# Longer convolution blocks, a reordered first load and two-instruction mixes in a convolution plus channel-mix kernel

## The chip, the cores and the metric

The kernel runs on one core of one Trainium2 chip. The metric is the device time of that core in microseconds (us), less is better. An execution counts as "fast" or "slow" by its state. The granted clock that is quoted for an execution is the mean share of full TensorE speed that the throttle allowed; in a single stretch it is 1.00 or 0.50.

## The reference

There are B = 8 batches of S = 4160 tokens with D = 192 channels. First a causal convolution over 7 taps, whose weights are softmaxed and shared by the 24 channels of each of 8 heads; then a channel mix with a hidden width of 1024.

```python
w = softmax(weight, axis=-1)                       # 8 heads x 7 taps
y[b, s, h*24+g] = sum_k w[h, k] * x[b, s + k - 6, h*24+g]
y_prev = y shifted by one token (zero at the start)
xk = mu_k * y + (1 - mu_k) * y_prev
xr = mu_r * y + (1 - mu_r) * y_prev
k = relu(xk @ w_k) ; v = (k * k) @ w_v             # 192 -> 1024 -> 192
out = sigmoid(xr @ w_r) * v
```

## The kernel before

The batches are worked in four pairs. The convolution is a matmul on TensorE: a block of 112 tokens and its halo of 6 earlier ones lies on the partitions of `xb`, and for every head one Toeplitz matrix `toe` with the seven weights on its diagonals multiplies it. Several blocks form a group. The tiles that matmuls write (`ps_...`) lie in PSUM, a memory apart from that of the other tiles. ScalarE evicts the result to `y` in bf16. `y` has tokens on its partitions and must be turned, so that channels are there: the first four groups of pair 0 go through TensorE transposes (`ps_t`, copied to `yT` by VectorE), all later ones through memory and a transposing DMA.

```python
BLK = 112 ; GB = 10 ; WARM = 34 ; P = 128 ; G = 24     # NBLK = 38 blocks a pair

# groups: (blocks, the step that needs them, turned on TensorE?)
((3, 0, True), (4, 1, True), (5, 2, True), (4, 3, True), (10, 4, False), (6, 6, False), (6, 7, False))
if p == 0
else ((10, 0, False), (10, 2, False), (9, 4, False), (9, 6, False))

def conv_mm(g, c, pool=None, tag="m"):
    ...
    ps = (pool or psM).tile([P, nb, 2, G * len(hs)], FP32, tag=tag, name="ps_c")   # psM holds two tiles
    for i, h in enumerate(hs):
        nc.tensor.matmul(out=ps[:BLK, :, :, i * G : (i + 1) * G], lhsT=toe[:, h, :],
                         rhs=xbs[g][:, :nb, :, h * G : (h + 1) * G], start=True, stop=True)
```

The main work is cut into steps of 512 tokens and, finer, into 260 slots. A slot is one k tile: 4 matmuls of 512 columns (8 of 256 in the short first and last step of pair 0) into `ps_k`, a ReLU eviction of 128x1024 by ScalarE (`k_sb`, 1.02 us), a square on VectorE (0.68 us). Beside it in each slot run matmuls of v and r of an earlier step. Pair 0 has slots 0 to 64, each later pair 65 more. The start of each `k_sb` eviction is the clock by which two traces can be laid side by side, and this text uses it so: "slot 12 is 0.72 us ahead" means that the 13th `k_sb` starts 0.72 us earlier than in the kernel before.

Between `yT` and k lies VectorE's part: a difference `d` of neighbouring tokens, then each mix as one instruction.

```python
nc.vector.scalar_tensor_tensor(out=o, in0=d[r0:r1, sl, :L], scalar=mu[r0:r1, i, part:part+1],
                               in1=yT[r0:r1, sl, c0:c0+L], op0=ALU.mult, op1=ALU.add)
```

The prologue warms TensorE with idle matmuls, writes the softmaxed rows to memory (`w_scr`) and reads them back diagonally as `toe`. DMAs named `nc.gpsimd` are issued by GpSimd, one after another.

```python
load_x(0) ; load_x(1)
nc.gpsimd.affine_select(out=ident, ...)
for _ in range(WARM): nc.tensor.matmul(out=warm, lhsT=ones_t, rhs=zeros, ...)
softmax()
nc.sync.dma_start(out=w_scr, in_=w_row)
load_toe() ; load_wk() ; load_x(2) ; load_wr() ; load_wv()
...
for t in tails: nc.gpsimd.memset(t, 0.0)
conv_mm(0, ...) ; conv_out(0, ...) ; tr_mm(0, ...) ; tr_out(0, ...)
conv_mm(1, ...) ; conv_out(1, ...)
diff(0) ; mix(0, ...) x4
for j in range(2): tr_mm(1, j) ; tr_out(1, j, dve_)
```

Later work stands in tables by slot. For groups turned on TensorE:

```python
per = 1
c0 = n0 - 14 if n0 > 12 else 1     # first convolution
r0 = c0 + nc_ + 1                  # first transpose; nc_ convolution pieces
```

## Time and profile before

| | before |
|---|---|
| median of six executions | 468.72 us (468.38 to 469.89) |
| profiled span | 467.2 us |
| TensorE busy (PE) | 445.2 us, 95% |
| VectorE busy (DVE) | 390.4 us, 84% |
| ScalarE busy (ACT) | 374.6 us, 80% |
| first convolution starts | 13.19 us |
| first `k_sb` starts | 20.90 us |
| granted clock 0.50 | 14.58 to 21.40 us |

TensorE is the bound of the steady state, and the first 20 us are a chain of waits with hardly any main work. The prediction below shows the lines.

### The profile page before, as it was taken

To read this page: it belongs to the slowest core of one execution; us is meant where nothing else is said; L and a number is where in the kernel's file an instruction comes from. 1 tells how busy PE (TensorE), PEld (TensorE's weight loads), DVE (VectorE), ACT (ScalarE), POOL (GpSimd) and SP (SyncE) were. 2 spreads that over 40 slices of the span, in tenths; PEclk is the share of its full clock that TensorE was granted. 3 is DMA by queue.
4 is the path that set the end of the run, shared out by engine and by line. 5 is a ranking of instruction groups with operands and counts; after the bars stand their busy time and mean duration, and the time that the engine had idled before them with its cause. 6 is when DMAs were issued, how large, how long until landed. Compare 5 with 4: busy or idle time off the path is not lost.

```text
span 467.2 us, 9868 instructions
## 1 busy us (share of the span) xinstructions
PE 445.2 (95%) x3892; PEld 300.6 (64%) x3954; DVE 390.4 (84%) x616; ACT 374.6 (80%) x549; POOL 51.1 (11%) x71
## 2 busy tenths in 40 slices
PE   7788999999999999999999999999999999999996
PEld 3454766666776666666676666666676666666676
DVE  2778988797998879889798989978898987999873
ACT  2489888988879797888879788888978888777771
POOL 5812211000010041000002041000002000000000
PEclk9799999999999999999999999999999999999999
DMA  7996699972459599945367679937157753511222
GB/s 89 160 174 106 162 197 156 233 200 68 127 142 183 148 139 229 181 129 139 93 173 119 165 133 214 229 100 187 52 152 138 173 135 100 153 65 56 69 69 94
DMA packets 138942, 65.79 MB, mean 141 GB/s; under 512 B 89936, under 2 KB 138464, under 8 KB 138896
## 3 DMA queue, kind: packets, MB, share of 16 engines
q1 hardware_dynamic: 98000, 49.26, 41.0%
q0 software_dynamic: 40896, 15.90, 30.0%
q8 instruction: 31, 0.51, 0.4%
q14 instruction: 15, 0.12, 0.1%
HBM read 31.59 MB, written 37.52 MB: 148 GB/s over the span
## 4 chain that ended last, share of the span: by engine, by line
PE 91%; ACT 2%; issue 2%; DMA 2%; DVE 1%; DVEq 0%; ACTq 0%
PE ps_k L343 38%; PE ps_v L433 37%; PE ps_c L199 5%; PE ps_r L416 5%; PE ps_r L415 5%; ACT k_sb L372 1%; DMA w_scr<-w_row 1%; PE ps_k L360 1%; DMA toe<-w_scr 1%; ACT y L219 1%; DMA w_raw<-in_weight_dram 1%; PE ps_t L257 1%; DVE yT L268 0%; ACT y L222 0%; DVE k L391 0%
## 5 line engine op out<-in xcount | busy, mean ns | idle before, releaser
L372 ACT ACTIVATE k_sb<-ps_k 128x1024 bf16<-128x1024 f32 x260 | 260.2, 1026 | 35.8 <-PE ps_k L343 31.8
L343 PE MATMUL ps_k<-xk,wk 64*128 64x512 bf16 (+2 forms) x994 | 206.0, 376 | 9.5 <-ACT k_sb L372 0.9
L433 PE MATMUL ps_v<-wv,k 128*128 128x192 bf16 x2048 | 210.8, 246 | 0.0
L433 PEld LDWEIGHTS <-k 128*128 128x128 bf16 x2048 | 175.4, 98 | 30.6 <-issue 1.4
L391 DVE TENSOR_TENSOR k<-k_sb 128x1024 bf16<-128x1024 bf16 x256 | 174.8, 684 | 16.7 <-ACT k_sb L372 16.0
L343 PEld LDWEIGHTS <-wk 64*128 64x128 bf16 (+1 forms) x1056 | 56.2, 96 | 109.2 <-issue 107.9
L446 DVE TENSOR_TENSOR o_sb<-ps_v,r_sb 128x384 f32<-128x384 f32 x132 | 72.2, 547 | 39.6 <-PE ps_v L433 34.7
L423 ACT ACTIVATE r_sb<-ps_r 128x384 bf16<-128x384 f32 x132 | 64.3, 487 | 38.1 <-PE ps_r L416 37.3
L301 DVE SCALAR_TENSOR_TENSOR xr<-d,mu,yT 128x1024 bf16<-128x1024 bf16 (+1 forms) x66 | 65.1, 988 | 0.1
L301 DVE SCALAR_TENSOR_TENSOR xk<-d,mu,yT 128x1024 bf16<-128x1024 bf16 (+1 forms) x66 | 64.4, 977 | 0.2
L415 PE MATMUL ps_r<-wr,xr 128*128 128x192 bf16 x256 | 62.8, 246 | 0.0
L416 PE MATMUL ps_r<-wr,xr 128*128 128x192 bf16 x256 | 62.8, 246 | 0.0
L219 ACT CAST y<-ps_c 112x480 bf16<-112x480 f32 (+4 forms) x100 | 47.9, 483 | 10.4 <-PE ps_c L199 10.2
L199 PE MATMUL ps_c<-xb,toe 128*112 128x480 bf16 (+5 forms) x152 | 46.2, 332 | 5.3 <-DMA toe<-w_scr 2.9
L109 POOL DMA_DIRECT2D xb<-in_x_dram x38 | 34.9, 928 | 26.8 <-PE ps_c L199 15.9
L281 DVE TENSOR_TENSOR d<-yT 128x1536 bf16<-128x1536 bf16 (+2 forms) x37 | 31.8, 859 | 0.4 <-DMA yT<-y_dram 0.2
L108 POOL DMA_DIRECT2D xb<-in_x_dram x8 | 4.3, 538 | 215.7 <-PE ps_k L343 206.3
L199 PEld LDWEIGHTS <-toe 128*112 128x112 bf16 x152 | 19.2, 134 | 12.1 <-DMA toe<-w_scr 3.4
L222 ACT CAST y<-ps_c 112x480 bf16<-112x480 f32 (+8 forms) x53 | 25.2, 482 | 0.2 <-DVE yT L227 0.2
L415 PEld LDWEIGHTS <-xr 128*128 128x128 bf16 x256 | 25.0, 98 | 0.0
L416 PEld LDWEIGHTS <-xr 128*128 128x128 bf16 x256 | 25.0, 98 | 0.0
L103 POOL DMA_DIRECT2D xb<-in_x_dram x8 | 4.6, 581 | 62.4 <-PE ps_r L416 61.0
(46 smaller groups left out, 67.8 us busy)
## 6 DMA issues: line engine op xcount, KB each, us to landing
out_dram<-o_sb SPq DMA_DIRECT2D x128, 192.0 KB, 2.3
y_dram<-y SPq DMA_DIRECT2D x7, 840.0 KB, 5.0
xb<-in_x_dram POOLq DMA_DIRECT2D x12, 432.0 KB, 12.0
y_dram<-y SPq DMA_DIRECT2D x6, 756.0 KB, 4.6
xb<-in_x_dram POOLq DMA_DIRECT2D x8, 480.0 KB, 13.2
xb<-in_x_dram POOLq DMA_DIRECT2D x6, 384.0 KB, 6.6
y_dram<-y SPq DMA_DIRECT2D x2, 504.0 KB, 10.7
xb<-in_x_dram POOLq DMA_DIRECT2D x4, 240.0 KB, 5.3
```

Source lines behind the costliest of these rows:

```text
L109: nc.gpsimd.dma_start(out=xb[:, lo:hi, s, :], in_=bass.AP(tensor=x.tensor, offset=x.offset + (b * S + t0 + lo * BLK) * D, ap=[[D, P], [BLK ...
L199: nc.tensor.matmul(out=ps[:BLK, :, :, i * G : (i + 1) * G], lhsT=toe[:, h, :], rhs=xbs[g][:, :nb, :, h * G : (h + 1) * G], start=True, sto ...
L219: copy(out=yh[:, :, :, c0 : c0 + n], in_=ps[:BLK, :, :, 0:n])
L301: nc.vector.scalar_tensor_tensor(out=o, in0=d[r0:r1, sl, :L], scalar=mu[r0:r1, i, part : part + 1], in1=yT[r0:r1, sl, c0 : c0 + L], op0=AL ...
L343: nc.tensor.matmul(out=ps[:, i, f * L : (f + 1) * L], lhsT=wk[r, 0 if hi else 1, fs], rhs=xk[r, i if hi else 2, :L], start=start and f == ...
L372: nc.scalar.activation(out=k_sb, in_=ps.rearrange("p a b -> p (a b)"), func=AF.Relu)
L391: nc.vector.tensor_tensor(out=o, in0=i, in1=i, op=ALU.mult)
L415: nc.tensor.matmul(out=o, lhsT=hi, rhs=wr[:, 0, :], start=True, stop=False)
L416: nc.tensor.matmul(out=o, lhsT=lo, rhs=wlo, start=False, stop=True)
L423: nc.scalar.activation(out=r_sb[:, :n, :], in_=ps[:, :n, :], func=AF.Sigmoid)
L433: nc.tensor.matmul(out=o, lhsT=k2[:, f, t * P : (t + 1) * P], rhs=wv[:, f, :], start=(f == 0), stop=(f == NF - 1),)
L446: nc.vector.tensor_tensor(out=o_sb[:, :n, :], in0=v_ps.pop(m)[:, :n, :], in1=r_sbs.pop(m)[:, :n, :], op=ALU.mult)
```

## The change

The intent: blocks of 120 tokens waste less of the 128 partitions on halo, so a pair needs 35 blocks, not 38. The Toeplitz matrix gets 128 columns. The second group's `x` is read behind the Toeplitz matrix instead of in front of it. Each mix becomes a scaling (tensor_scalar) and an in-place addition (tensor_tensor). The groups and the slots of the early transposes are rearranged, and six warm-up matmuls are added.

```diff
-    BLK = 112
+    BLK = 120
-    WARM = 34
+    WARM = 40
-            ((3, 0, True), (4, 1, True), (5, 2, True), (4, 3, True), (10, 4, False), (6, 6, False), (6, 7, False))
+            ((3, 0, True), (4, 1, True), (4, 2, True), (5, 3, True), (10, 4, False), (6, 6, False), (3, 8, False))
-            else ((10, 0, False), (10, 2, False), (9, 4, False), (9, 6, False))
+            else ((10, 0, False), (8, 2, False), (8, 4, False), (9, 6, False))
-    toe = const.tile([P, H, BLK], BF16)
+    toe = const.tile([P, H, P], BF16)
-                out=ps[:BLK, :, :, i * G : (i + 1) * G],
+                out=ps[:, :, :, i * G : (i + 1) * G],
@@ mix
-        elif part == 0:
-            go(t[:, 0:2, :L], slice(0, 2), 0, P)
         else:
-            go(t[:, 2, :L], 2, 0, P)
+            sl = slice(0, 2) if part == 0 else slice(2, 3)
+            o = t[:, sl, :L]
+            nc.vector.tensor_scalar(
+                out=o, in0=d[:, sl, :L], scalar1=mu[:, i, part : part + 1], scalar2=None, op0=ALU.mult
+            )
+            nc.vector.tensor_tensor(out=o, in0=o, in1=yT[:, sl, c0 : c0 + L], op=ALU.add)
@@ schedule
-            r0 = c0 + nc_ + 1
+            r0 = c0 + nc_
@@ prologue
         load_x(0)
-        load_x(1)
...
         load_toe()
+        load_x(1)
         load_wk()
```

Cut here: the padding of `yT` to a multiple of 16, the clipping of the transposing read at S, and the width of the Toeplitz read.

## The prediction

> **What bounds the kernel now.** I read the page's busy shares first, then the chain that ended last, then the same engines stretch by stretch, and last the chain and the timeline of the first 23 us.
>
> ```profile
> PE 445.2 (95%) x3892; PEld 300.6 (64%) x3954; DVE 390.4 (84%) x616; ACT 374.6 (80%) x549; POOL 51.1 (11%) x71
> PE 91%; ACT 2%; issue 2%; DMA 2%; DVE 1%; DVEq 0%; ACTq 0%
> ```
>
> TensorE is busy 95% of 467.2 us and carries 91% of the chain. VectorE at 84% is near, so the average alone doesn't say whether VectorE's part of the change can pay. The windows table (busy us of each engine in a stretch) does:
>
> ```profile
> 0.00:13.20 13.20, 8.95 (x35) 3.68 (x35) 2.39 (x10) 3.02 (x4) 8.27 (x17) 1.00 0.75 101
> 13.20:19.30 6.10, 4.55 (x38) 3.64 (x39) 4.23 (x10) 2.73 (x8) 6.07 (x10) 0.61 1.34 171
> 19.30:43.00 23.70, 19.86 (x152) 11.37 (x155) 20.10 (x31) 19.59 (x33) 7.20 (x10) 0.96 1.03 127
> ...
> 131.00:240.35 109.35, 107.05 (x938) 72.17 (x954) 95.63 (x149) 92.62 (x134) 9.84 (x12) 1.00 0.76 153
> ```
>
> Columns are PE, PEld, DVE, ACT, POOL, then granted clock, DMA share and GB/s. The last row is one pair of batches in the steady state: PE 107.05 of 109.35, VectorE 95.63, so there only TensorE's own work counts. In 19.3 to 43 all three compute engines are near 20 of 23.7: a start-up stage with mixed limits. Before 19.3 nothing of the main work runs; what sets that part is the chain:
>
> ```profile
> 5.21 4.21 DMA w_scr<-w_row
> 9.42 0.29 issue
> 9.71 3.44 DMA toe<-w_scr
> 13.15 0.04 issue
> 13.19 0.60 PE ps_c L199 x6
> ...
> 16.10 0.49 PE ps_c L199 x2
> ...
> 18.35 1.11 PE ps_t L257 x10
> 19.46 1.41 PE ps_k L343 x8
> 20.88 0.02 issue
> 20.90 1.02 ACT k_sb L372
> ```
>
> The softmaxed weights go out to memory (4.21 us) and come back as the Toeplitz matrix (3.44 us); from the first convolution to the first large matmul are about 6 us more, of alternating convolution, eviction and transposition. The DMA records say why the write takes 4.21 us: its 2048-byte packets run from about 7.2 to 8.9 us, while the x packets of group 1 run from 6.4 to 10.2 us beside them.
>
> **What the Trainium skill says.** "VectorE: DVE Perf Modes", section "The perf-mode tier table", puts tensor_scalar on bf16 in SBUF at four elements a cycle (693 ns for 2048) and tensor_tensor at two (1224 ns). For tensor_tensor this trace agrees: the square of 1024 elements takes 684 ns, the difference of 1536 takes 956 ns, which is half the elements at 0.96 GHz plus about 0.15 us. The trace holds no tensor_scalar. The present mix (scalar_tensor_tensor) takes 1279 ns for 1024 and 735 for 512, 1.06 ns an element: one a cycle.
> "TensorE: Matmul & The Clock Gate", section "Weight-path perf modes", says the fast weight load is on when the number of weights is 128. The trace fits: loads of toe with 112 columns take 134 ns, loads of 128 columns 98 ns.
> The same page, section "Part 1: The HAM clock gate", says TensorE falls to half rate after an idle window of about 3.4 us. Here the warm-up matmuls end at 10.3, toe lands at 13.15, and the granted clock is 0.5 from 14.6 to 21.4 us, two such windows; the 8 matmuls of 192 columns at 16.1 took 1.44 us.
>
> **The change part by part.**
> (1) Blocks of 120. A pair of batches needs 35 blocks in place of 38. Every block costs 2 x 192 = 384 streamed columns, so 3 x 4 x 384 = 4608 columns go. In the steady chain the convolution matmul of 432 columns stands with 0.18 us, so 0.417 ns a column: 4608 x 0.417 = 1.92 us, of which 0.48 us in each pair. This is on the path wherever TensorE is the bound, which is nearly everywhere past 43 us. I book -1.9.
> (2) Weight loads of toe with 128 columns: 152 x 36 ns = 5.5 us off PEld. In the steady chain the matmuls follow one another with no gap for the load (k for 1.51 us, convolution 0.18, v at once), so it is hidden. I book 0.
> (3) Mixes. By the skill's four a cycle and the trace's fixed 0.15 us, I estimate a tensor_scalar of 1024 at 256/0.96 + 150 = 0.42 us and of 512 at 0.28. The addition takes 0.68 and about 0.42. Consecutive independent instructions on VectorE start some 0.08 us before the last one's recorded end, dependent ones 0.04 after it. So 1024: before 1.20 a piece, after 0.42 + 0.04 + 0.60 = 1.06; 512: before 0.66, after 0.28 + 0.04 + 0.34 = 0.66. A step of 512 tokens holds two of each: 2 x 0.14 = 0.3 us saved of some 12 us VectorE work, about 9 us in the 31 full steps. In the steady state VectorE waits for TensorE anyway: 0 there. In start-up, where the chain passes an xr mix at 39.95, perhaps 0.2. VectorE's busy time should come out near 380 to 388.
> (4) Group 1's x behind the Toeplitz matrix. Without x packets beside them, 128 packets of 2048 B at 0.09 us on 16 engines are under 0.8 us in place of 1.7. So w_scr should land at about 8.5 (not 9.42) and toe, issued at 8.8, with rows of 256 B in place of 224 B, at about 12.2 to 12.4 (not 13.15): -0.9 up to here. The price: both x transfers of group 1 are issued by 11.5, and their 1024 packets need some 2.4 us at the rate of the trace (about 220 in half a microsecond) after toe's data at 11.8, so they land near 15. The second convolution would want them at 16.1 - 0.9 = 15.2. That is tight: a delay of up to 0.7 is possible. The wk load moves behind them and lands near 17.9, and the first large matmul wants it at 18.4. I book -0.7 with these chances in it.
> (5) Warm-up 40 in place of 34: 6 x 0.213 = 1.3 us more, to 11.6. They end before toe lands, so they delay nothing, and the idle gap shrinks from 2.9 to about 0.7 us. If the clock stays at full rate, 10 transposes (1.11) and 8 k matmuls (1.41) on the chain halve: 1.2 us. But between 12 and 18 us TensorE is busy less than half the time, so another window may count as idle. I give it 4 in 10: -0.5.
> (6) Groups 2 and 3 swap four and five blocks, transposes come one slot earlier. ScalarE's evictions of group 2 shrink by a fifth (five copies, about 0.3 us) in slots 2 to 5, where the chain runs through its k_sb, and grow again in group 3. I book -0.3 with the 0.2 of (3), and see it as the least certain.
> Sum: -1.9 - 0.7 - 0.5 - 0.3 = -3.4, so 468.9 - 3.4 = 465.5 us.
>
> **The rivals.**
> (a) tensor_scalar with a per-partition scalar in memory does not get the fast mode. At one element a cycle it costs 1.22 us for 1024 and 0.69 for 512. Per step VectorE would gain 2 x (1.22 + 0.04 + 0.60 - 1.20) + 2 x (0.69 + 0.04 + 0.34 - 0.66) = 2.1 us, on some 11.7; a step of TensorE is 13.3. VectorE becomes the bound: 13.8 a step, some 33 x 0.5 = 16 us more, about 482. For it: no run here shows the instruction. Against it: the skill's table, and the fixed mode rule that tensor_tensor obeys here.
> (b) The prologue's gain is eaten by the wait that takes its place: x of group 1 or wk lands late and the first k matmul starts at 19.3 or later. For it: GpSimd issues one DMA after another from 10 to 22 us without a pause, and all use one queue. Against it: the x transfers keep 3 us of slack before the second convolution. Time: about 466.7.
> (c) The clock stays up through the whole prologue and start-up loses its knots: another 1.5 us, about 463.5.
> (d) The convolution columns saved don't shorten the chain, because VectorE or ScalarE sets the step. For it: VectorE is busy 87% of the steady window. Against it: TensorE is busy 98% there. Time: 467.4.
>
> **Range and chances.** The convolution's 1.9 is firm. The rest is between +0.3 and -3.5, so 462.9 to 467.3 should hold it 8 times in 10. The 2% marks are at 459.5 and 478.3. Going below the first needs 6 us more than the sum and I see no source; going above the second needs rival (a). Chances: faster 0.03, same 0.94, slower 0.03.
>
> **What would show it.** Right: PE busy in a steady pair falls from 107.05 by about 0.5, and the pair lasts about 108.8; toe lands near 12.3; the first k matmul starts at 18.2 to 18.8; tensor_scalar of 1024 takes near 0.42 us and VectorE's total falls slightly. Wrong: tensor_scalar near 1.2 us with waits of TensorE for xk; a wait of the second convolution for the x DMA beyond 0.7 us; a steady pair still at 109.3; or a w_scr write that still takes over 4 us with no x traffic beside it, so that contention was not its cause.

## More of the kernel before

One caution for all readings of busy time: the ends of matmuls are modelled, and of the 1056 k matmuls this trace holds records of 994. So the starts of `k_sb`, which are recorded on ScalarE, are the safer measure of progress.

## The result, and the profile after

| | before | after |
|---|---|---|
| median of six executions | 468.72 us (468.38 to 469.89) | 466.12 us (465.89 to 466.96) |
| ratio (95% interval) | | 0.9946 (0.9932 to 0.996) |
| profiled span | 467.2 us | 464.4 us |

A ratio is the mean time of one kernel's fast runs over that of the other's of the same rounds, so it is not quite the ratio of the medians. The change saves about half a per cent: "same" by the 2% mark, 0.6 us from the predicted 465.5 and inside the range.

The page of the kernel after, its busy line and the shares of the chain that ended last:

```profile
PE 445.4 (96%) x3898; PEld 298.3 (64%) x3960; DVE 387.3 (83%) x748; ACT 371.3 (80%) x544; POOL 49.5 (11%) x71
PE 91%; DMA 2%; DVE 2%; ACT 2%; issue 2%; POOL 0%; DVEq 0%
```

Nothing changed in kind: TensorE still carries 91%. VectorE lost 3.1 us of busy time while it got 132 more instructions.

The start in the same stretches as before (columns: PE, PEld, DVE, ACT, POOL busy; granted clock, DMA share, GB/s):

```profile
0.00:13.20 13.20, 11.03 (x51) 5.00 (x52) 2.93 (x12) 4.08 (x7) 8.58 (x18) 1.00 0.58 83
13.20:19.30 6.10, 4.50 (x35) 3.10 (x37) 5.28 (x14) 1.69 (x5) 4.30 (x8) 0.61 1.37 192
19.30:43.00 23.70, 19.57 (x153) 11.01 (x153) 19.36 (x36) 20.52 (x34) 5.40 (x7) 0.96 0.98 123
```

PE has 2.08 us more in the first row, the six extra warm-up matmuls and a convolution that now begins inside it. The clock column stands at 0.61 and 0.96 exactly as before: the half-speed stretch did not go away, it lies at 14.52 to 21.35 us.

The chain that ended last, from the write of the softmaxed rows on (start, length, what):

```profile
5.22 2.35 DMA w_scr<-w_row
7.57 0.29 issue
7.86 0.61 POOL toe L174
8.47 0.72 POOL xb L109
9.19 5.52 DMA xb<-in_x_dram
14.71 0.14 issue
14.85 0.49 PE ps_c L199 x2
```

The write took 2.35 us in place of 4.21 us. `toe` was issued at 7.86 and landed 3.1 us later, so at about 11.0. It is no longer on the chain: the reading of group 1's `x` (5.52 us, landed at 14.71) took its place, and TensorE waited 1.2 us for it. The second convolution began at 14.85 in place of 16.10, the first `k_sb` at 19.73 in place of 20.90.

How long one pair takes is read from the tail slots that end pairs 0 and 1. ScalarE's evictions that waited for the tail's k matmuls, first of the kernel before (start, length, engine, what, idle before it and its releaser):

```profile
129.97 1.02 ACT L372 ACTIVATE k_sb<-ps_k 128x1024 bf16<-128x1024 f32 x1 [0.40 <-PE ps_k L360]
239.20 1.02 ACT L372 ACTIVATE k_sb<-ps_k 128x1024 bf16<-128x1024 f32 x1 [0.40 <-PE ps_k L360]
```

and of the kernel after:

```profile
128.40 1.02 ACT L375 ACTIVATE k_sb<-ps_k 128x1024 bf16<-128x1024 f32 x1 [0.40 <-PE ps_k L363]
237.09 1.02 ACT L375 ACTIVATE k_sb<-ps_k 128x1024 bf16<-128x1024 f32 x1 [0.40 <-PE ps_k L363]
```

The differences are 109.23 and 108.69: 0.54 us less in a steady pair.

Read this way slot by slot, the lead of the kernel after is:

| slot | 0 | 4 | 8 | 10 | 12 | 65 | 130 | 195 | 259 (last) |
|---|---|---|---|---|---|---|---|---|---|
| lead, us | 1.17 | 1.02 | 1.78 | 1.88 | 0.72 | 1.57 | 2.11 | 2.66 | 2.84 |

So it gains 1.17 us before the first k tile, another 0.7 us up to slot 10, loses 1.16 us between slots 10 and 12, and then gains 2.12 us up to the end. The rise before slot 10 and the fall after it belong together: counted from slot 4 (1.02) to slot 12 (0.72), 0.30 us are lost. After slot 12 the gain goes with the blocks saved: 0.85 us up to slot 65 (five blocks), 0.54 in each of the next two pairs (three blocks), 0.18 in the last, where one block is left, because by the slot tables two of its three run ahead in the pair before.

### The profile page after: what moved, and what is told of

It is laid out like the page before. It is cut to its first block, busy times and chain, and to the rows that moved or that the text cites. A ratio compares the mean times of both kernels' runs of the same rounds, so it can differ in the third digit from the quotient of the medians.

```text
span 464.4 us, 10001 instructions
## 1 busy us (share of the span) xinstructions
PE 445.4 (96%) x3898; PEld 298.3 (64%) x3960; DVE 387.3 (83%) x748; ACT 371.3 (80%) x544; POOL 49.5 (11%) x71
## 4 chain that ended last, share of the span: by engine, by line
PE 91%; DMA 2%; DVE 2%; ACT 2%; issue 2%; POOL 0%; DVEq 0%
PE ps_k L346 39%; PE ps_v L436 37%; PE ps_r L418 5%; PE ps_r L419 5%; PE ps_c L199 4%; DMA xb<-in_x_dram 1%; ACT k_sb L375 1%; PE ps_k L363 1%; DMA w_raw<-in_weight_dram 1%; ACT y L219 1%; PE ps_t L257 1%; DMA w_scr<-w_row 1%; DVE k L394 0%; ACT y L222 0%; DVE yT L268 0%
## 5 line engine op out<-in xcount | busy, mean ns | idle before, releaser
L426 ACT ACTIVATE r_sb<-ps_r 128x384 bf16<-128x384 f32 x132 | 64.4, 488 | 39.3 <-PE ps_r L419 38.8
L219 ACT CAST y<-ps_c 120x384 bf16<-120x384 f32 (+4 forms) x96 | 45.0, 471 | 8.8 <-PE ps_c L199 8.8
L199 PE MATMUL ps_c<-xb,toe 128*128 128x384 bf16 (+6 forms) x152 | 43.5, 321 | 4.1 <-ACT y L222 1.8
L323 DVE TENSOR_TENSOR xr<-xr,yT 128x1024 bf16<-128x1024 bf16 (+1 forms) x66 | 36.2, 549 | 2.3
L323 DVE TENSOR_TENSOR xk<-xk,yT 128x1024 bf16<-128x1024 bf16 (+1 forms) x66 | 36.2, 549 | 2.3
L109 POOL DMA_DIRECT2D xb<-in_x_dram x38 | 33.5, 888 | 31.0 <-issue 17.5
L320 DVE TENSOR_SCALAR xr<-d,mu 128x1024 bf16<-128x1024 bf16 (+1 forms) x66 | 27.9, 423 | 0.1
L108 POOL DMA_DIRECT2D xb<-in_x_dram x8 | 4.4, 552 | 221.1 <-PE ps_k L346 221.1
L320 DVE TENSOR_SCALAR xk<-d,mu 128x1024 bf16<-128x1024 bf16 (+1 forms) x66 | 26.6, 403 | 0.2
L222 ACT CAST y<-ps_c 120x384 bf16<-120x384 f32 (+9 forms) x52 | 24.0, 466 | 0.4 <-DVE yT L227 0.2
```

Of the source, the lines that this page charges most:

```text
L199: nc.tensor.matmul(out=ps[:, :, :, i * G : (i + 1) * G], lhsT=toe[:, h, :], rhs=xbs[g][:, :nb, :, h * G : (h + 1) * G], start=True, stop=True,
L219: copy(out=yh[:, :, :, c0 : c0 + n], in_=ps[:BLK, :, :, 0:n])
L320: nc.vector.tensor_scalar(out=o, in0=d[:, sl, :L], scalar1=mu[:, i, part : part + 1], scalar2=None, op0=ALU.mult)
L323: nc.vector.tensor_tensor(out=o, in0=o, in1=yT[:, sl, c0 : c0 + L], op=ALU.add)
L426: nc.scalar.activation(out=r_sb[:, :n, :], in_=ps[:, :n, :], func=AF.Sigmoid)
```

## The experiments

Theory after reading the traces: the steady gain is the convolution columns; the start's gain comes from the quiet write; the rearranged groups and slots give it back between slots 10 and 12; the mixes bring nothing; the half clock stayed because TensorE idles in small pieces. Rivals: the gain of the steady part comes from the narrower weight loads or from VectorE's relief; the late `x` of group 1 is what keeps the start long; the loss at slots 10 to 12 is the clock's doing.

Twelve kernels ran in four calls, each call on one chip with its own runs of the kernel before (medians 469.35, 469.23, 469.22, 469.60). All gave correct results. A "lead" below is that of the one profiled execution of a kernel. "To the end" in the leads is slot 259.

### The parts one by one

**e1_x_order**: the kernel before, with only the order of the loads changed.

```diff
         load_x(0)
-        load_x(1)
...
         load_toe()
+        load_x(1)
         load_wk()
```

> The kernel before with group 1's x read after the Toeplitz matrix, and nothing else (warm-up stays at 34). Theory: the write of w_scr takes about 2.4 us in place of 4.2, but the second convolution then waits about 1 us for its x, as in the changed kernel: the first large eviction (k_sb, 20.90 us in the kernel before) comes at about 19.7. The clock is half until about 21.4 whatever the order, and the start-up stage gives back 0.2 to 0.5, so the time is 0.7 to 1.0 us less (ratio about 0.998). Rival: the wait for x eats all of it, the first k_sb comes at 20.7 or later and the time is the same within 0.3 us.

Measured: 468.19 us, ratio 0.997 (0.9954 to 0.9986). Its chain:

```profile
5.53 2.21 DMA w_scr<-w_row
...
9.70 5.96 DMA xb<-in_x_dram
```

The write is 2.0 us shorter than before here too, so the `x` packets beside it were its cost: their place is the one thing that was changed. But it began 0.3 us later (5.53 for 5.21), and the chain runs on through the `x` transfer, which lands at 15.66, so that only 0.44 us arrive at the first `k_sb`, which starts at 20.46 and not at the expected 19.7. That lead stays: 0.52 us at slot 12 and 0.52 at the end. No loss at slots 10 to 12. The ratio says more, 0.003 x 469.35 = 1.4 us. The half clock, whose place differs from run to run (the section on the clock), can make such a difference; that it did was not tested.

**e2_blocks**: the kernel after without its mixes, load order and warm-up, that is, blocks, groups and slots alone.

```diff
-    WARM = 40
+    WARM = 34
         load_x(0)
+        load_x(1)
...
-        load_x(1)
@@ mix: the single scalar_tensor_tensor of the kernel before
```

> The changed kernel without the new order of x, without the split mixes and with 34 warm-up matmuls: blocks of 120, the new groups and transposes one slot earlier alone. Theory: 4608 columns less on a TensorE that is the bound: from slot 12 to the end the evictions k_sb gain about 2.1 us on the kernel before, of them about 0.55 in each later pair; up to slot 12 they gain nothing (within 0.3 us). Time 1.8 to 2.3 us less. Rival: the shorter weight loads or ScalarE's smaller evictions also count, then more than 2.5 us; or the columns are hidden behind VectorE, then under 1 us.

Measured: 467.36 us, ratio 0.9955 (0.9942 to 0.9968), 2.1 us less. The profiled execution was the slowest of the six (468.48 us at a mean clock of 0.988; the others 466.59 to 467.41): it had a second half-clock stretch from 42.8 to 46.2 us. Its lead went from 1.13 us at slot 10 to 0.92 us behind at slot 12 and 1.67 behind at slot 16, and from there to 0.44 ahead at the end: 2.11 us. So the steady gain belongs to the blocks (here with the 128-column `toe`, which e8_120col takes out), without any help of the mixes. A loss between slots 10 and 12 is here as well, larger, but the clock muddies its size. The expectation that nothing is gained up to slot 12 missed: the profile was 1.04 us ahead at slot 8, before that stretch began, and behind at slot 12.

**e3_mix**: the kernel before, with only the mixes changed (the mix part of the diff above).

> The kernel before with the mixes as scaling plus addition, and nothing else. Theory: a tensor_scalar of 1024 takes 0.49 us and the dependent addition starts only after it, so a mix costs VectorE as much as before; VectorE's busy time changes by less than 3 us and the time by less than 0.4 us either way. Rival: relief of VectorE pays in the start-up stage: 0.5 to 1 us less.

Measured: 469.67 us, ratio 1.0009 (0.9996 to 1.0022). VectorE is busy 388.9 us, 1.5 us less, and the time is no shorter. The profile is 1.3 us behind from slot 4 to the end and level in between, with 10.2 us of half clock and one stalled instruction, of which more below. By the ratio the split mixes alone are worth nothing: at best 0.2 us gained, at worst 1 us lost.

The groups by shape show what the instructions cost. The kernel before (line, engine, operation, output and input, shapes, count; then busy us, mean ns of one, idle before them):

```profile
L301 DVE SCALAR_TENSOR_TENSOR xk<-d,mu,yT 128x1024 bf16<-128x1024 bf16 x31 | 39.6, 1279 | 0.2
```

and the kernel after:

```profile
L320 DVE TENSOR_SCALAR xk<-d,mu 128x1024 bf16<-128x1024 bf16 x31 | 15.2, 489 | 0.2
L323 DVE TENSOR_TENSOR xk<-xk,yT 128x1024 bf16<-128x1024 bf16 x31 | 21.6, 696 | 1.1
...
L320 DVE TENSOR_SCALAR xr<-d,mu 128x512 bf16<-128x512 bf16 x33 | 11.9, 360 | 0.0
```

The fast mode is there: 489 ns for 1024 elements, not the 1220 ns of one element a cycle. But 489 + 696 = 1185 ns against 1279 ns leaves little, and the addition needs the scaling's result, which costs a small gap each time. Over all mixes the page's groups go from 65.1 + 64.4 = 129.5 us to 36.2 + 36.2 + 27.9 + 26.6 = 126.9 us busy, with 4.6 us of idle time just ahead of the additions. That is a wash.

**e8_120col**: the kernel after with 120 columns in `toe`, so that the weight loads are not 128 wide.

```diff
-    toe = const.tile([P, H, P], BF16)
+    toe = const.tile([P, H, BLK], BF16)
-                out=ps[:, :, :, i * G : (i + 1) * G],
+                out=ps[:BLK, :, :, i * G : (i + 1) * G],
```

Cut here: the read of `toe`, 120 wide as well.

> The changed kernel with a Toeplitz matrix of 120 columns in place of 128, so that its weight loads take about 134 ns again and not 101. Theory: the loads are hidden behind the matmul before, the time is the same within 0.4 us (the read of toe may come 0.1 us earlier or later). Rival: the loads are on the path: 152 x 33 ns = 5 us more at most, 0.5 us or more if a tenth of them is.

Measured: 466.84 us, ratio 0.9943 (0.9931 to 0.9956), which is the kernel after's. Its group of weight loads:

```profile
L199 PEld LDWEIGHTS <-toe 128*120 128x120 bf16 x152 | 18.9, 134 | 8.7 <-issue 1.3 <-PE ps_c L199 0.2
```

and that of the kernel after:

```profile
L199 PEld LDWEIGHTS <-toe 128*128 128x128 bf16 x152 | 14.8, 101 | 9.6 <-issue 1.8 <-PE ps_c L199 0.2
```

The load is 33 ns longer again, 152 times, and nothing of it reaches the end: from slot 12 to the end both gain 2.12 us. The loads are hidden.

**e6_double**: the kernel after with every convolution matmul of pairs 1 to 3 issued twice (the result stays right, the second overwrites the first).

```diff
-        for i, h in enumerate(hs):
+        for i, h in enumerate([h for h in hs for _ in range(2 if groups[g][0] > 0 else 1)]):
+            i = h - hs[0]
```

> The changed kernel with every convolution matmul of batch pairs 1 to 3 issued twice (same result): 3 x 35 x 384 = 40320 columns more. Theory: a column streamed is 0.417 ns on the path, so the time is 16.8 us more (16 to 18), ratio to the kernel before about 1.030. Rival: VectorE or ScalarE sets the step, and TensorE has slack: under 10 us more.

Measured: 483.21 us, ratio 1.0293 (1.0276 to 1.0311), as expected. The same two evictions as above:

```profile
130.55 1.02 ACT L376 ACTIVATE k_sb<-ps_k 128x1024 bf16<-128x1024 f32 x1 [0.40 <-PE ps_k L364]
244.78 1.02 ACT L376 ACTIVATE k_sb<-ps_k 128x1024 bf16<-128x1024 f32 x1 [0.40 <-PE ps_k L364]
```

A steady pair takes 114.24 us (the lines are rounded), 5.55 us more than the 108.69 of the kernel after, for 35 x 384 = 13440 more columns: 0.413 ns a column, fully on the path. By that price the 3 x 384 = 1152 columns that the change takes off a pair are worth 0.48 us. Measured are 0.54; what makes up the other 0.06 to 0.07 us is open.

### The start

**e4_old_start**: the kernel after with the old grouping of groups 2 and 3 and the old transpose slots.

```diff
-((3, 0, True), (4, 1, True), (4, 2, True), (5, 3, True), ...
+((3, 0, True), (4, 1, True), (5, 2, True), (4, 3, True), ...
-            r0 = c0 + nc_
+            r0 = c0 + nc_ + 1
```

> The changed kernel with groups 2 and 3 of five and four blocks again and the transposes one slot later, as in the kernel before. In the changed kernel the lead over the kernel before grows to 1.9 us at slots 8 to 10 and falls to 0.72 at slot 12. Theory: the new schedule crowds the transposes of group 3 (three of them, from slot 10) into the same bundle as the convolutions of group 4, which wait for PSUM; with the old schedule the lead of about 1.0 from the prologue stays at slot 12, so the time is about 0.3 us less than the changed kernel's. Rival: the knot at slots 10 to 12 comes from the mixes or from the blocks, and the old schedule changes nothing or loses 0.3 to 1 us.

Measured: 467.01 us, ratio 0.994 (0.9922 to 0.9957). By the two ratios it is 0.3 us less than the kernel after, as expected, but far inside the intervals, so the time tells nothing. The lead of about 1.0 us that was expected at slot 12 did not come: it is 0.12. The profile tells two things. Between slots 10 and 12 nothing is lost (0.12 us ahead at both). But the start's lead of 0.77 us at slot 0 had already melted to 0.15 at slot 8. The likely reason is one tensor_scalar of 512 elements, which takes 0.35 us elsewhere and took 1.84 us at 17.51. One of the runs, at a granted clock of 1.0, took 464.93 us. So the test of the schedule was spoilt, and the next runs take out what probably spoilt it.

**e5_fill**: the kernel after with idle matmuls on the warm-up tile between the small pieces of the start.

```diff
-        for _ in range(WARM):
-            nc.tensor.matmul(out=warm, lhsT=ones_t, rhs=zeros, start=True, stop=True)
+        spin(WARM)                 # spin(n): n such matmuls
...                                  # conv_mm(0, ...)
+        spin(3)
...                                  # conv_out(0), tr_mm(0), tr_out(0)
+        spin(5)
...                                  # conv_mm(1), conv_out(1)
+        spin(4)
         diff(0)
```

> The changed kernel with twelve more idle matmuls on the warm-up tile, in TensorE's gaps of the prologue: 3 after the first convolution, 5 after the first transposes, 4 after the second convolution. Theory: the half clock (3.4, 6.8 or 10.2 us long in the profiles so far, at a place that differs from run to run) comes from these gaps. With them filled it does not come before the end of the kernel; transposes and first k matmuls run at full rate, k_sb 0 comes 0.5 to 1 us earlier than in the changed kernel (19.73), the time is 0.5 to 1.2 us less (464.9 to 465.6 on a chip where the changed kernel takes 466.1) and the spread of its runs narrows. Rival: the clock goes by something else, or the fillers delay the work they stand before: no half-clock stretch goes, or the time is the same or more.

Measured: 466.66 us, ratio 0.9942 (0.9929 to 0.9956). The clock did what the theory said: all executions at 0.998 to 1.0, no half-clock stretch in the start. The first `k_sb` is 2.07 us ahead. The time is still no better than the kernel after's. Where it went is in two places: the lead is down to 1.23 us at slot 4, and from 1.42 at slot 10 it falls to 0.28 at slot 12. The second is the same loss as in the kernel after, now at full clock, so the clock is not its cause. The first is this, in VectorE's timeline:

```profile
17.58 1.90 DVE L320 TENSOR_SCALAR xr<-d,mu 128x256 bf16<-128x256 bf16 x1
```

with GpSimd at the same time:

```profile
17.47 0.93 POOL L154 DMA_DIRECT2D wv<-in_moe_w_v_dram  x1
18.39 1.01 POOL L558 MEMSET tail<- 128x512 bf16 x2
```

The scaling ends at 19.48, just after the two memsets of `tails` end at 19.40. "SBUF — State Buffer" of the Trainium skill, section "SBUF: two separate sides", says that VectorE in a two-port mode and GpSimd share a pair of ports as an exclusive lock: whichever starts first keeps it for its whole instruction and the other is blocked. In e3_mix and e4_old_start a tensor_scalar of 512 elements was drawn out to 1.72 and 1.84 us at the same memsets. One thing does not fit the page: by the records the scaling started first, 0.81 us before the first memset (0.46 and 0.68 in the other two), and was held all the same. Spans on GpSimd are rough, so which of the two had the ports first is not shown. In the profile of the kernel after itself the small mixes were just through when the memsets began at 18.46, and none was stalled.

**e9_fill_tails**: e5_fill with those memsets moved to the front of GpSimd's work, before the Toeplitz read.

```diff
         nc.gpsimd.affine_select(out=ident, ...)
+        for t in tails:
+            nc.gpsimd.memset(t, 0.0)
...
-        for t in tails:
-            nc.gpsimd.memset(t, 0.0)
```

> The kernel with filled gaps (e5_fill), and GpSimd's two memsets of the tail tiles moved into its idle stretch before the Toeplitz read. In e5_fill one tensor_scalar of 256 elements took 1.90 us (17.58 to 19.48) instead of 0.28, while GpSimd issued a DMA (to 18.40) and ran these memsets (18.39 to 19.40); in e3_mix one took 1.72 us beside the same memsets. Theory: tensor_scalar and a GpSimd instruction cannot run side by side, and the memsets held it. Without them there, no tensor_scalar before 25 us takes over 0.7 us, and the lead over the kernel before, 2.07 us at k_sb 0 and only 1.23 at k_sb 4 in e5_fill, is at least 1.7 at k_sb 4; time 0 to 0.8 us less than e5_fill. Rival: the DMA issue alone holds it, and a tensor_scalar of over 1.2 us stays.

Measured: 465.58 us, ratio 0.9928 (0.9909 to 0.9946). The same instruction in its trace:

```profile
18.06 0.28 DVE L320 TENSOR_SCALAR xr<-d,mu 128x256 bf16<-128x256 bf16 x1
```

The issue of the `wv` DMA (17.93 to 18.86) still lies beside it, begun 0.13 us before it as in e5_fill (0.11), and doesn't hold it. So the hold needs the memsets. That the port is the means is the page's account; no run here tests it. The lead is 1.92 us at slot 4 in place of 1.23, and 2.16 at slot 10; then again it drops, to 1.01 at slot 12.

**e7_kfirst**: the kernel after, with the transposes of group 1 moved behind the first two k tiles, so that the late `x` can't hold those.

```diff
-        for j in range(2):
-            tr_mm(1, j)
-            tr_out(1, j, dve_)
@@ slot table
+    for j in range(2):
+        pe.setdefault(0, []).insert(j, (tr_mm, (1, j)))
+        dve.setdefault(0, []).insert(j, (tr_out, (1, j, nc.vector.tensor_copy)))
```

> The changed kernel with the transposes of group 1 moved behind the first two slots of k matmuls, which do not need them. In the changed kernel the chain runs from the x of group 1 (landing 14.71) through convolution, evictions, transposes to the first k matmul at 18.08. Theory: the late x is then beside the path: the first k matmul comes right after the second convolution, at 16.3 to 16.8, k_sb 0 at 17.5 to 18.2 (not 19.73), and as ScalarE bounds the first slots, 0.5 to 1.5 us of it reach the end. Rival: step 1's mixes, which wait for those transposes, now come later and hold slot 4: the lead is gone by slot 5 and the time is the same.

Measured: 467.26 us, ratio 0.995 (0.9937 to 0.9964). The first `k_sb` is 2.06 us ahead, 0.9 us more than in the kernel after, and nothing of that is left soon: 0.87 at slot 4, 1.00 at slot 8, 0.06 behind at slot 12, 2.07 at the end. The wait for `x` can be taken off the first k tile, but what follows it, the copies to `yT`, the next `d` and its mixes on VectorE, is not earlier. In fact those copies start at 20.13 us in place of 17.73, and at slot 4 the lead is below the 1.02 of the kernel after, much as the rival had it. So an earlier first k tile alone is worth nothing. The rival that the late `x` keeps the start-up long is not settled by this, because group 1's own work was put later too.

**e10_one_mix**: the kernel after with the single mix instruction.

> The changed kernel with the mixes in one instruction again, as in the kernel before: the split undone in the finished kernel. Theory: split and single mixes cost VectorE the same (busy time within 4 us), so the time is the same as the changed kernel's within 0.5 us, ratio to the kernel before 0.9935 to 0.9955. Rival: the split is what pays in the changed kernel, then at least 1 us more; or it costs by the waits for GpSimd, then up to 1 us less.

Measured: 466.8 us, ratio 0.9959 (0.9938 to 0.9981). It lies between the two expectations and its interval spans the kernel after's 0.9946. VectorE is busy 389.7 us. It has the drop too: 1.55 us ahead at slot 10, 0.11 at slot 12. So the split mixes don't cause the drop, and whether they give or take half a microsecond can't be told.

**e11_combined** and **e12_old_split**: e9_fill_tails with the old groups and transpose slots of e4_old_start; e11 has single mixes, e12 the split ones.

```diff
-((3, 0, True), (4, 1, True), (4, 2, True), (5, 3, True), ...
+((3, 0, True), (4, 1, True), (5, 2, True), (4, 3, True), ...
-            r0 = c0 + nc_
+            r0 = c0 + nc_ + 1
@@ e11_combined only: the single scalar_tensor_tensor in mix
```

> A candidate to beat both: the changed kernel with single mixes, the old groups 2 and 3 and old transposition slots, filled gaps and the moved memsets. Theory: with single mixes and the old schedule e1_x_order kept all of its prologue lead (0.44 us at k_sb 0, 0.52 at slot 12), so here the lead of about 2 us at k_sb 0 stays to slot 12, and 2.1 us of the columns come on top: about 4 us less than the kernel before, ratio 0.991 to 0.992. Rival: slots 4 to 12 are bound by VectorE and ScalarE alone and swallow a lead above 0.7 us: ratio 0.994 as in the changed kernel.

> The combined candidate with the mixes split again: the changed kernel with the old groups 2 and 3 and old transposition slots, filled gaps and moved memsets. It tells which of the two kept the lead of 1.85 us at slot 12 in the combined candidate, where the filled kernel with the new schedule kept 1.01. Theory: the schedule did; with the memsets moved, split mixes cost what single ones do, and the lead at slot 12 is 1.6 to 2.0 us, time within 0.4 us of the combined candidate. Rival: the single mixes did; the lead at slot 12 is 1.2 us or less.

Measured: e11 465.58 us, ratio 0.9926 (0.9907 to 0.9946), a little short of its expectation; e12 465.08 us (464.68 to 466.01), ratio 0.991 (0.9896 to 0.9923). Its lead at slot 12, 1.84 us, is what the theory had; its time is 0.5 us below that of e11, where 0.4 had been allowed. The leads:

| slot | 0 | 4 | 8 | 10 | 12 | 259 |
|---|---|---|---|---|---|---|
| after | 1.17 | 1.02 | 1.78 | 1.88 | 0.72 | 2.84 |
| e9 (new groups, full clock, no stall) | 1.59 | 1.92 | 2.07 | 2.16 | 1.01 | 3.13 |
| e11 (old groups, single mixes) | 1.88 | 2.00 | 1.91 | 1.88 | 1.85 | 3.54 |
| e12 (old groups, split mixes) | 1.83 | 1.91 | 1.86 | 1.83 | 1.84 | 3.96 |

With the old groups the drop is gone: the lead that the start makes is carried whole to slot 12, and in e12 2.12 us are added to it as in the kernel after. Up to slot 12 the two mixes can't be told apart (1.85 and 1.84). e11 adds only 1.69 us after that; it falls behind e12 between slots 26 and 31, where one v matmul waits 0.2 us for VectorE's `o_sb`, a wait that e12's trace does not have.

This holds in every profile: in the eight with the new groups and slots, slot 12 loses 1.14 to 2.05 us on slot 10, in the five other ones with the old at most 0.03. The cleanest pair is e9 and e12, which differ in nothing else: level at slot 4, 0.83 us apart at slot 12. The times of the runs would not have shown it: e9 and e11 ran on one chip and have the same median, 465.58 us, e12 ran on another, and the intervals of the three overlap.

What the drop is shows in TensorE's waits between 36 and 44 us, where slots 10 to 13 lie (us in total, times, longest). The kernel before:

```profile
PE ps_c L199 <- ACT y L222: 0.9, 1, 0.9
PE ps_t L257 <- ACT y L219: 0.4, 1, 0.4
PE ps_c L199 <- DVE yT L268: 0.2, 1, 0.2
```

and the kernel after:

```profile
PE ps_c L199 <- ACT y L222: 1.3, 2, 1.0
PE ps_c L199 <- DVE yT L268: 1.2, 2, 0.7
```

In e12 the three lines of before are back, with the same figures. Group 3 has five blocks in the change, so three transposes instead of two, and they begin at slot 10, where the convolutions of the ten-block group 4 are under way (slots 8 to 11). Both use the two `psM` tiles. The wait of 1.0 us for ScalarE's `y` was there before too, with 0.9. The longest of the new ones, for VectorE's `yT`, in TensorE's timeline:

```profile
39.55 0.47 PE L257 MATMUL ps_t<-ident,y 120*128 120x120 bf16 x6
...
41.50 0.36 PE L199 MATMUL ps_c<-xb,toe 128*128 128x480 bf16 x1 [0.74 <-DVE yT L268]
```

and in VectorE's:

```profile
39.70 0.70 DVE L323 TENSOR_TENSOR xr<-xr,yT 128x1024 bf16<-128x1024 bf16 x1
40.31 0.69 DVE L394 TENSOR_TENSOR k<-k_sb 128x1024 bf16<-128x1024 bf16 x1
40.91 0.53 DVE L268 COPY yT<-ps_t 128x720 bf16<-128x720 bf16 x1
```

The transposes are done at 40.02. VectorE copies them out at 40.91, behind a mix and a square that come first in its order, and the convolution that wants the tile begins at 41.50.

e12 beats both kernels: about 0.009 x 469.6 = 4.2 us less than the kernel before, and by the two ratios (0.991 against 0.9946) about 1.7 us less than the kernel after. The two ratios are from different chips and rounds; their intervals do not touch.

### The clock

The half-clock stretches of all profiles were laid beside TensorE's busy time in stretches of 3.41 us, on the grid at which the clock changes. The kernel after (PE busy is the first figure behind the length, the granted clock the third from the end):

```profile
11.11:14.52 3.41, 1.80 (x20) 1.08 (x17) 1.46 (x5) 1.06 (x3) 3.07 (x5) 1.00 1.20 137
14.52:17.94 3.42, 2.65 (x19) 2.01 (x20) 3.10 (x10) 1.69 (x5) 1.96 (x4) 0.50 1.30 198
```

and e12_old_split:

```profile
12.83:16.24 3.41, 3.15 (x28) 1.91 (x26) 2.26 (x7) 1.32 (x5) 2.17 (x4) 1.00 1.29 200
```

In the kernel after TensorE was busy 1.80 of 3.41 us, 53%, and ran at half speed in the next stretch. In e12 it was busy 3.15 of 3.41 in the stretch with the same small pieces, and full speed stayed in the next one. The kernel before had 0.87 of 3.42 us ahead of its own. Up to the last 10 us of the profiles, every change to half speed followed a stretch with a busy share of 0.21 to 0.56, and those of 0.57 or more were followed by full speed. But three of 0.55 to 0.56 stayed at full speed too (in the kernel after, e7_kfirst and e6_double), and in the last 10 us two of 0.43 and 0.44 did (e1_x_order, e7_kfirst). So there is no sharp mark: below 0.40 half speed always followed, from 0.43 to 0.56 sometimes, above that never. Back to full speed it went only after a stretch of 0.93 or more; 0.71 to 0.87 did not do it. These are shares of modelled busy time, so the figures are rough. The place of the grid differs from run to run, and so the same kernel is hit or not: the kernel before took 467.4 to 467.6 us where its clock was 0.998, and 468.9 to 470.4 us at 0.988 to 0.993.

## Why the prediction was right or wrong

The total, 465.5 us, was right to 0.6 us; its terms were right in part, so some of the nearness is luck: 0.5 us booked for the clock did not come, and the columns and the start brought more than was booked. In the profiles: -1.17 up to the first `k_sb`, +0.45 up to slot 12, -2.12 from there; sum -2.84, against -3.4 predicted.

- **(1) Columns, -1.9: right.** Measured -2.12, or 0.54 in a steady pair for 0.48 predicted. e6_double confirms the price, 0.413 ns a column, and with it that rival (d) was wrong: convolution columns are on the path. The predicted sign in the busy time did not show: TensorE's busy time in a pair fell by 0.15 us only, from 107.04 to 106.89, and the rest came out of gaps. With modelled ends that split means little; the pair's length is what counts.
- **(2) Weight loads, 0: right.** e8_120col has the slower loads and the same time.
- **(3) Mixes, 0.3 us a step: the mechanism right, the size off.** The fast mode is on, so rival (a) fell. But the term "256/0.96 + 150 = 0.42 us" measured 0.49, and the one for 512, 0.28, measured 0.36. With that the two instructions of a mix cost about what the one did: in a steady pair VectorE is busy 94.61 us in place of 95.51, 0.11 us less a step and not 0.3. The prediction also had no term for the port that GpSimd and a tensor_scalar contend for: 1.4 to 1.6 us in the profiles where the memsets meet a mix.
- **(4) Group 1's `x` behind `toe`, -0.7: the mechanism right, its parts mis-sized, the sum near.** The write took 2.35 us where 3.3 were booked (the landing at 8.5): by the DMA records its packets took 1.2 us in place of 2.2, a saving of 1.0 where 0.9 was booked, and the first one came 0.8 us after the issue in place of 1.7, for which the sum had no term. `toe` landed at 11.0 where 12.2 to 12.4 were. The `x` landed at 14.71, near the predicted 15, and was waited for, as "tight" said; 1.2 us rather than up to 0.7. The first k matmul began at 18.08, just ahead of the predicted 18.2 to 18.8. The first `k_sb` is 1.17 us ahead; of this e1_x_order explains 0.44 by the order alone, and e2_blocks has 0.43 without the order, so the two together do not quite give it. Single profiles of the start differ by tenths with the place of the half clock. The wait of rival (b) is thus real, but it did not eat the gain.
- **(5) Clock, -0.5 as 4 chances in 10: did not happen.** The step "if the clock stays at full rate" rested on closing the gap before the first convolution. That gap was closed and the half clock came all the same, because the small pieces after it leave TensorE idle nearly half of the time; the prediction had named this doubt. Filling those holes (e5_fill) removed the half clock in every execution. Rival (c) is a true possibility, but a change of this kind doesn't bring it.
- **(6) Groups and slots, -0.3 with the 0.2 of (3): failed.** The step counted a fifth less eviction in slots 2 to 5 and let them "grow again in group 3" at no cost. A gain is there, 0.7 us up to slot 10, and then 1.16 us are lost; from slot 0 to slot 12 that is 0.45 us lost in place of 0.3 gained. The third transpose of group 3 meets group 4's convolutions at two PSUM tiles. e11_combined and e12_old_split, with the old groups and slots, keep the lead.

Two sums of the prediction do not come out: 465.5 less the 1.5 of rival (c) is 464.0, not 463.5, and the 1.9 with a rest of -3.5 puts the lower end of the range at 463.5, not 462.9. The measured time lies inside either range.

What stays open: the 0.06 to 0.07 us a pair beyond the columns; the sign of the mixes' small effect; and which of the two parts, the five blocks of group 3 or the earlier transpose slots, makes the drop, as they were only undone together; and, last, what the late `x` of group 1 costs the start-up.

## What to carry to other kernels

In a kernel that one engine bounds, columns taken off that engine paid by their count here, and relief for engines that wait (VectorE, the weight loads) paid nothing; a split of one instruction in two has to be priced with its fixed parts and with the engine that shares its port. A start-up made of small pieces should be judged by the start of a late tile and not by the first: e5_fill and e7_kfirst had 2.1 us at the first k tile and at most 0.28 us twelve slots later. Holes between small matmuls can cost the clock; idle matmuls put into them kept it up here.

## What the Trainium skill lacked or had wrong

- "TensorE: Matmul & The Clock Gate", section "Part 1: The HAM clock gate": it speaks of an idle window of about 3.4 us. The length agrees with every half-clock stretch that ends inside a profile (3.41 us and multiples). But it gives no busy share at which a window counts as idle, and a window need not be wholly idle: one with TensorE busy 1.80 of 3.41 us was enough for half speed, and one of 71 to 87% busy did not bring full speed back, one of 93% did.
- "VectorE: DVE Perf Modes", section "The perf-mode tier table": the fast mode of tensor_scalar with a per-partition scalar holds, but 1024 elements took 489 ns. Four elements a cycle at 0.96 GHz are 267 ns of that, so the fixed part is about 0.22 us. The page's 693 ns for 2048 leave 0.16 us by the same reckoning. The single mix (scalar_tensor_tensor) has no row in that table; it measured 1279 ns for 1024 here.
- "SBUF — State Buffer", section "SBUF: two separate sides": an exclusive lock fits what was seen: beside two GpSimd memsets of 1.01 us together a tensor_scalar was drawn out from 0.28 to 1.90 us. But "starts first" does not fit the records as they stand, in which the tensor_scalar starts 0.81 us before the memsets.
- No page has, as far as was looked, a figure for what a small write costs beside reads that GpSimd issued: 256 KB took 4.21 us with them and 2.35 us without.
